# Small vectors loaded as rows, one product of eight on GpSimd, five inverses of eight on summed tiles, the MLP's flips in one PSUM tile, and a new order: a gated long convolution and a gMLP on one core

## The chip, the cores and the metric

The kernel runs on one core of one Trainium2 chip. The metric is the device time of one execution in microseconds (us); times of before are the median of three runs. Names in the profile: PE is TensorE (matmuls), PEld its weight loads, DVE VectorE, ACT ScalarE, POOL GpSimd, SP the engine that only issues DMAs; SPq and ACTq are their DMA issues.

## The reference

A block of two parts with adaptive layer norm (six modulation vectors sa, ca, ga, sb, cb, gb from `silu(c) @ w_mod`); S = 2048 rows, D = 640 channels, Fh = 864. All inputs are bfloat16.

```python
h = layernorm(x) * (1 + ca) + sa
k_shift = sum over t of k shifted by t rows * shift_k[:, t]      # four taps
kv = k_shift * v
y  = causal convolution of kv with ssm_k along S (by FFT)  +  kv * ssm_D
x  = x + ga * (h * y)
h  = layernorm(x) * (1 + cb) + sb
z  = gelu(h @ w_in);  z1, z2 = halves of z;  z2 = layernorm(z2)
g  = w_sp @ z2 + b_sp                                            # mixes the rows
x  = x + gb * ((z1 * g) @ w_out)
```

## The kernel before

**Stages.** The channels are cut into NU = 5 units u of 128. For each unit the filter (K side) and kv (U side) are transformed on TensorE: `stage1` (line 401 on) multiplies 16-row blocks with the small table F1 into a tile X1, `forward` (fwdK, fwdU) multiplies X1 with the tables M2, eight steps st per unit, each with six matmuls. A K step is copied to SBUF by ACT (khc, tile KH). A U step stays in PSUM (pu) and DVE multiplies it with KH into four partial products of 128x1024 elements (`prod`, line 457). The inverse (`inv`) multiplies with the tables G2 into pz, and a copy (zc) collects Z. For the steps in SUMS (1, 3, 5, 7) the partial products are written as float32 (tile Tf), two row sums (`csum`, line 466, POOL or DVE) reduce them to W, and the inverse takes six matmuls on W; for the other steps they are bfloat16 (tile T) and the inverse takes twelve on T.

Z of units 0 to 3 is transposed by one DMA (`zt`, line 673) into ZT, of which there is one buffer; four y steps (`y`, eight matmuls each, and `ym` on DVE) end it and multiply it into gh, the modulated layer norm of x (`ghm`, two operations for each unit and group of four row tiles, on POOL or DVE). `res` adds gh to x, `ln2` takes statistics for the second norm. Unit 4 is turned by PE instead (`zfl`, copies `zk`, then `yl`, `yml`).

**Inputs.** kv is made channel-wise: `ldk` loads k and v by DMA transpose (line 511), `diag` (line 528) makes four diagonal matrices from the four taps of a channel tile dt, `taps` multiplies with them, `tv` multiplies with v, `kvw` writes kv to DRAM, and `ldX` (line 386) reads filters (XK) and kv (XU) back in the layout of stage 1. Unit 0's XU needs both halves of dt0's write. ssm_D is added to XK (`addD`, line 396) from the tile D_col. D, the taps and c are loaded straight into partition layout, one element or four to a descriptor (lines 733, 736, 737).

**MLP.** Groups g of four row tiles. `zx` normalises, then group 0 (in two pieces p of two row tiles) is turned by PE (`hfl`) and modulated out of PSUM (`hmod`); groups 1 to 3 are turned by DMA (`turn`) and modulated in SBUF (`hmod2`). `zz` multiplies with w_in, `gelu` follows on ACT, `stz`, `agz`, `rstdz`, `zn` normalise z2. The mixing with w_sp (line 944) and the projection (line 965) come after, outside the list.

**The order.** Every operation is registered with `op(engines, kind, function, reads, writes)` and gets a number. The list ORDER names, in one line of text, which engine issues which number; an engine issues its own entries in the order of the list, and semaphores hold an instruction until its inputs and its buffer are there. SP's entries too run in their own order: a DMA whose input is late holds back those behind it. PSUM tags with their buffers: s1 (1), sm, pu, pz (2 each). FILLS are matmuls on the identity whose results nobody reads (`fill`, tag s1). `silut` and `gelut` are one-element activations that load ACT's tables for Silu (also used for the sines) and Gelu.

## Time and profile before

| | us |
|---|---|
| three runs | 325.06, 324.6, 325.04; median 325.04 |
| profiled execution, its time / its span | 324.96 / 323.0 |
| PE / DVE / ACT / POOL busy | 308.3 / 209.8 / 148.3 / 93.4 |
| first stage-1 block of U0 | starts at 26.03 |
| ZT transposes issued at | 60.07, 84.26, 99.69, 114.29 |
| first MLP matmul (zz) | starts at 136.16 |
| mixing with w_sp begins | 195.4 |

A span runs from the first to the last instruction; the execution's time is 2 us longer. A group line of the profile reads: line, engine, operation, tiles written <- read, shapes, count | busy us, mean ns of one | idle time of the engine before them and what ended it. In windows and in the list of instructions the first two numbers are start and length in us. Line 240 is the helper `mm`, line 243 the helper `copy`: their groups are told apart by the tiles.

### The profile page before, as it was taken

The numbers are of one execution on the slowest core, as the hardware profiler recorded it, in microseconds if no ns is written. First come the engines' busy times: TensorE is split into PE (matmuls) and PEld (weight loads), VectorE is DVE, ScalarE is ACT, GpSimd is POOL, SyncE is SP. The second block draws the span as 40 slices with busy tenths as digits, with TensorE's granted clock in tenths as the row PEclk, the third lists the DMA queues.
The fourth block names the chain that finished last, engine by engine and source line by source line (L and its number), as shares of the span: only waits on it lengthen the run. The fifth ranks groups of instructions, "written<-read, shape, count | busy, mean of one in ns | idle before, by whom it ended". The sixth has DMA issues, their size and how long they took to land.

```text
span 323.0 us, 6384 instructions
## 1 busy us (share of the span) xinstructions
PE 308.3 (95%) x2581; PEld 205.8 (64%) x2589; DVE 209.8 (65%) x464; ACT 148.3 (46%) x255; POOL 93.4 (29%) x121
## 2 busy tenths in 40 slices
PE   5969999899999998899999999999999999999996
PEld 2556879778889896655555555555555555555554
DVE  8967999999999998899676773433322222233333
ACT  4757999897779755397577683000000000000001
POOL 2440725559799898310111120000000000000000
PEclk9989999999999999999999999999999999999999
DMA  6999997996687876004308980567655555522231
GB/s 114 224 255 275 244 282 187 245 244 170 118 230 152 264 140 231 4 1 81 74 9 141 193 214 2 118 136 110 141 130 124 114 114 115 114 51 49 49 51 61
DMA packets 128868, 44.99 MB, mean 139 GB/s; under 512 B 117992, under 2 KB 128072, under 8 KB 128840
## 3 DMA queue, kind: packets, MB, share of 16 engines
q1 hardware_dynamic: 125672, 41.74, 59.0%
q10 hardware_dynamic: 3168, 2.86, 2.7%
q8 instruction: 20, 0.33, 0.4%
q14 instruction: 8, 0.07, 0.1%
HBM read 16.11 MB, written 5.24 MB: 66 GB/s over the span
## 4 chain that ended last, share of the span: by engine, by line
PE 76%; DMA 10%; DVE 7%; SPq 4%; issue 1%; ACT 1%; POOL 0%; POOLq 0%; DVEq 0%
PE ps L944 29%; PE pu L240 16%; PE pz L240 13%; PE po L965 9%; PE sm L240 5%; DMA ZT<-Z 5%; DMA X<-in_A_ssm_k_dram 5%; SPq L511 3%; PE s L240 3%; DVE Tf L457 1%; DVE X L243 1%; DVE st L570 1%; DVE T L457 1%; PE sm L823 0%; DVE big L543 0%
## 5 line engine op out<-in xcount | busy, mean ns | idle before, releaser
L944 PE MATMUL ps<-X,wT 128*128 128x432 bf16 x512 | 95.7, 346 | 0.0
L944 PEld LDWEIGHTS <-wT 128*128 128x128 bf16 x512 | 50.0, 98 | 42.2
L957 ACT COPY uT<-pt 128x896 bf16<-128x896 bf16 x1 | 0.9, 905 | 119.1 <-PE pt L956 119.1
L240 PE MATMUL pu<-X,M 128*128 128x128 bf16 (+1 forms) x480 | 47.1, 240 | 1.5 <-DVE T L457 0.9
L240 PEld LDWEIGHTS <-Z 128*128 128x128 bf16 x320 | 31.1, 98 | 26.6 <-DVE Z L832 0.4
L240 PEld LDWEIGHTS <-M 128*128 128x128 bf16 x480 | 37.8, 99 | 7.2 <-issue 1.8
L947 DVE SCALAR_TENSOR_TENSOR u<-ps,bcol,G 128x432 bf16<-128x432 f32 x18 | 12.0, 668 | 42.2 <-PE ps L944 42.2
L243 ACT CAST X<-s 128x1024 bf16<-128x1024 f32 x32 | 32.7, 1021 | 4.4 <-PE s L240 4.3
L965 PE MATMUL po<-w_o,uT 128*128 128x320 bf16 (+2 forms) x231 | 33.2, 295 | 0.1
L240 PE MATMUL pu<-big,Z 128*128 128x432 bf16 x160 | 32.8, 346 | 0.0
L466 POOL TENSOR_TENSOR W<-Tf 128x256 bf16<-128x256 f32 x38 | 28.0, 756 | 16.4 <-DVE Tf L457 15.6
L240 PE MATMUL pz<-big,Z 128*128 128x432 bf16 x160 | 32.6, 346 | 0.0
L947 DVE SCALAR_TENSOR_TENSOR u<-ps,bcol,M 128x432 bf16<-128x432 f32 x14 | 9.3, 667 | 30.2 <-PE ps L944 30.2
L965 PEld LDWEIGHTS <-uT 128*128 128x128 bf16 (+1 forms) x231 | 22.2, 98 | 9.9 <-issue 0.2
L240 PEld LDWEIGHTS <-G 128*128 128x128 bf16 x360 | 26.9, 98 | 1.9
L243 ACT CAST KH<-pu 128x512 bf16<-128x512 f32 x40 | 23.0, 595 | 6.7 <-PE pu L240 6.5
L457 DVE TENSOR_TENSOR Tf<-pu,KH 128x1024 f32<-128x1024 f32 x20 | 24.2, 1219 | 1.6 <-PE pu L240 1.1
L457 DVE TENSOR_TENSOR T<-pu,KH 128x1024 bf16<-128x1024 f32 x20 | 24.3, 1217 | 0.6 <-PE pu L240 0.5
L967 DVE TENSOR_TENSOR ot<-po,xt 128x320 bf16<-128x320 f32 (+1 forms) x33 | 15.9, 482 | 12.6 <-PE po L965 12.6
L243 ACT CAST Z<-pz 128x512 bf16<-128x512 f32 x35 | 20.3, 589 | 6.7 <-PE pz L240 6.4
L240 PEld LDWEIGHTS <-X 128*128 128x128 bf16 x288 | 18.1, 98 | 8.0 <-DVE X L396 4.5
L888 DVE BATCH_NORM_STATS2 stz<-X 128x6 f32<-128x432 bf16 x32 | 18.2, 594 | 7.1 <-ACT X L882 7.1
(143 smaller groups left out, 411.5 us busy)
## 6 DMA issues: line engine op xcount, KB each, us to landing
wm<-in_w_mod_dram SPq DMA_DIRECT2D x4, 800.0 KB, 5.6
out_dram<-ot SPq DMA_DIRECT2D x15, 160.0 KB, 2.3
big<-in_B_w_in_dram SPq DMA_DIRECT2D x2, 1080.0 KB, 8.3
X<-in_A_ssm_k_dram SPq DMA_DIRECT2D x4, 512.0 KB, 6.2
kv_scr<-big SPq DMA_DIRECT2D x4, 512.0 KB, 3.6
X<-kv_scr SPq DMA_DIRECT2D x4, 512.0 KB, 5.4
xt<-in_A_q_dram SPq DMA_DIRECT2D x3, 640.0 KB, 6.6
wm<-in_w_mod_dram ACTq DMA_DIRECT2D x2, 800.0 KB, 7.3
```

The costliest lines, as they stand in the source:

```text
L240: nc.tensor.matmul(o, lhsT=w, rhs=x, start=start, stop=stop)
L243: (e.copy if e is nc.scalar else e.tensor_copy)(dst, src)
L457: e.tensor_tensor(T_[:], tl[pu][:, :, :, None, :].to_broadcast([P, KP, 2, 2, DU]), tl[KH][:, :, None, :, :].to_broadcast([P, KP, 2, 2, DU] ...
L466: e.tensor_tensor(tl[W][:, :, o, :], T_[:, :, 0, o, :], T_[:, :, 1, 1 - o, :], op=ALU.add if o else ALU.subtract)
L511: e.dma_start_transpose(tl[name][:, o + h * m:o + (h + 1) * m], src[0, h * m:(h + 1) * m, dt * P:(dt + 1) * P])
L570: e.bn_stats(out=st[:, a, :], in_=xt[:, n, a * HS:(a + 1) * HS])
L888: op("D", "stz", lambda e, i=i, n=n, fc=fc: e.bn_stats(out=stz[:, n, fc, :], in_=tl[z2][:, i, fc * FC:(fc + 1) * FC]), r=[(z2, (i, fc))], ...
L944: nc.tensor.matmul(ps[:, :FC], lhsT=wTs[t][:, s_, :], rhs=tl["z2_%d" % (s_ // TB)][:, s_ % TB, fc * FC:(fc + 1) * FC], start=(s_ == 0), st ...
L947: nc.vector.scalar_tensor_tensor(u[:, sl], ps[:, :FC], bcol[:, t:t + 1], z1[t][:, sl], op0=ALU.add, op1=ALU.mult)
L957: nc.scalar.copy(uTs[t][:], pt[:])
L965: nc.tensor.matmul(ps[:, :hi - lo], lhsT=uTs[t][:fsz[ft], ft, :], rhs=w_o[:fsz[ft], ft, lo:hi], start=(ft == 0), stop=(ft == NFT - 1))
L967: nc.vector.tensor_tensor(ot[:, lo:hi], ps[:, :hi - lo], xt[:, t, lo:hi], op=ALU.add)
```

## The change

**Small vectors.** c, the taps and D are loaded as rows (5 x 128, 5 x 128 x 4, 80 x 8 elements, tag KH), turned by TensorE against the identity into PSUM (tag sm), and copied out; D is first widened on DVE or POOL into a zeroed tile of 80 x 128, so that its turned form has zeros where D_col had them. Silu reads c from PSUM. The memset of D_col goes.

**Steps.** MODE replaces SUMS: steps 0, 1, 3, 5, 7 of each unit are summed ("s"), 4 and 6 are not ("u"), and for step 2 ("p") ACT copies the forward tile pu to SBUF as float32 (`puc`) and POOL makes the product in bfloat16 (`prg`); its inverse takes twelve matmuls.

**Flips.** The five channel tiles of a piece of group 0 are turned into one PSUM tile (tag s1, one buffer) instead of five tiles of tag sm.

**Fills.** Seven (4, 2, 1, 1, 4, 1, 4 matmuls) instead of three (4, 1, 4).

**The list** is new. Entries by engine, before to after, where the numbers differ (the larger kinds):

| kind | before | after |
|---|---|---|
| prod | DVE 40 | DVE 35; puc ACT 5, prg POOL 5 |
| csum | POOL 38, DVE 2 | POOL 44, DVE 6 |
| ghm | POOL 27, DVE 13 | POOL 20, DVE 20 |
| res (units 0 to 3 and 4) | POOL 7, DVE 14 | POOL 3, DVE 18 |
| s1c | ACT 44, DVE 4 | ACT 41, DVE 7 |
| zc | ACT 35, DVE 5 | ACT 37, DVE 3 |
| zn | ACT 5, DVE 11 | ACT 7, DVE 9 |
| ln1 / xn | ACT 5, DVE 11 / ACT 4, DVE 12 | ACT 6, DVE 10 / ACT 3, DVE 13 |
| mneg, msgn, gneg, diag | POOL 2, 3, 3, 4; DVE 2, 1, 1, 1 | POOL 2, 4, 4, 3; ACT 2, 0, 0, 1; DVE 0, 0, 0, 1 |

Its start, decoded: SP before: D, taps, k and v of dt0 in halves (with XK0's second half between), x rows 0, k of dt1, XK1, kv write of dt0's second half, v of dt1, XU0, k of dt2. SP after: XK0's second half, D as rows, k and v of dt0 (first halves), XK1, k and v of dt0 (second halves), x rows 0, k of dt1, the kv write, v of dt1, XU0, k of dt2. ACT before: XK0's first half, silut, cosines, sines and copies, kv write of dt0's first half. ACT after: taps as rows, silut, XK0's first half, copy of the taps, dt0's diag (four multiplications), cosines, sines and copies, the same kv write. PE after: fill x4, turn of the taps, fill x2, turn of D, fill, taps dt0, fill, stage 1 of K0, of K1 (one block), taps dt0, the forwards of K0 with the other three blocks of K1 among them, taps dt1, stage 1 of U0. PE before had one block of K1 ahead of U0.

Its PE entries between the last y of a unit and the first y of the next:

| between | before | after |
|---|---|---|
| units 0 and 1 | 9 forwards, 4 stage-1, 2 u, 1 s, 3 taps | 7 forwards, 3 stage-1, 1 u, 1 p, 2 s, 1 taps |
| units 1 and 2 | 6 forwards, 4 stage-1, 3 u, 1 s, modulation columns | 7 forwards, 4 stage-1, 2 u, 3 s |
| units 2 and 3 | 7 forwards, 3 u, 3 s, modulation columns | 7 forwards, 2 u, 4 s, modulation columns |

(u, p, s: inverses of that kind.) In unit 4, after: inverse 4.0, inverse 4.3, forward 4.2, two more forwards, inverses 4.4, 4.5, 4.7, 4.6 with two forwards among them, y of unit 3, inverse 4.2, inverse 4.1; POOL meanwhile: a residual, row sums of 4.7 and 4.5, a gate operation, a row sum of 4.5, the product 4.2, a row sum of 4.1. Behind the last y of unit 3 come fill x4, fill x1 and the first yl; then, before the first hfl, fill x4. The first Gelu is behind two zx on ACT; `gelut`, which stood in unit 3, comes after 19 Gelus.

```diff
@@ -31,57 +31,58 @@
-FILLS = (4, 1, 4, )
-SUMS = (1, 3, 5, 7)
+FILLS = (4, 2, 1, 1, 4, 1, 4, )
+MODE = ('sspsusus', 'sspsusus', 'sspsusus', 'sspsusus', 'sspsusus')
 SLOTS = dict(Tf=2, W=2, X=3, X1=4, KH=9, T=3, Z=3, ZT=1, wm=1, big=2, dg=2, st1=2, s1=1, sm=2, pu=2, pz=2)
 PSUM_TAGS = ("s1", "sm", "pu", "pz")
 
 
 ORDER = """
...
 """
 
 
@@ -159,7 +160,6 @@
     x_nat = A_q[0].rearrange("(n p) d -> p n d", p=P)
     out_nat = out[0].rearrange("(n p) d -> p n d", p=P)
     ssm_fft = A_ssm_k.rearrange("(c g) (n f) -> (g n) c f", g=8, f=P)
-    d_fft = A_ssm_D.rearrange("(c g) -> g c", g=8)
     wmv = w_mod.rearrange("(t p) (j d) -> p t j d", p=P, j=6)
 
 
@@ -212,8 +212,6 @@
         gsa_bf = consta.tile([P, D], BF16)
         D_col = consta.tile([P, D // 8], BF16)
         sk = consta.tile([P, ND, 4], F32)
-        sk_bf = consta.tile([P, ND, 4], BF16)
-        c_bf = consta.tile([P, ND], BF16)
         sc = consta.tile([P, ND], F32)
         sc_rep = consta.tile([P, ND, P], BF16)
         sc_bf = consta.tile([P, ND], BF16)
@@ -266,7 +264,6 @@
         nc.gpsimd.iota(pint[:], [[0, 1]], base=0, channel_multiplier=1)
         nc.gpsimd.iota(pidx[:], [[0, 1]], base=0, channel_multiplier=1, allow_small_or_imprecise_dtypes=True)
         nc.gpsimd.iota(fidx[:], [[1, P]], base=0, channel_multiplier=0, allow_small_or_imprecise_dtypes=True)
-        nc.gpsimd.memset(D_col[:], 0.0)
         nc.gpsimd.iota(f1k[:], [[4, NKC], [0, 2]], base=1, channel_multiplier=0, allow_small_or_imprecise_dtypes=True)
         nc.gpsimd.iota(f1r[:], [[0, NKC], [16, 2]], base=48, channel_multiplier=0, allow_small_or_imprecise_dtypes=True)
         nc.gpsimd.memset(mpi[:], -2.0 * HALF_PI)
@@ -449,14 +446,20 @@
             pu, KH, T, pz, Z = "pu" + s, "KH" + s, "T" + s, "pz" + s, "Z%d" % u
             forward(pu, "X1U%d" % u, st)
 
-            summed = st in SUMS
-            ttag = "Tf" if summed else "T"
-
-            def product(e):
-                T_ = new(T, ttag, [P, KP, 2, 2, DU], F32 if summed else BF16)
-                e.tensor_tensor(T_[:], tl[pu][:, :, :, None, :].to_broadcast([P, KP, 2, 2, DU]),
-                                tl[KH][:, :, None, :, :].to_broadcast([P, KP, 2, 2, DU]), op=ALU.mult)
-            op("D", "prod", product, r=[pu, KH], w=[T], new=[(T, ttag)])
+            mode = MODE[u][st]
+            summed = mode == "s"
+            shape = [P, KP, 2, 2, DU]
+
+            def product(e, src=None):
+                T_ = new(T, "Tf" if summed else "T", shape, F32 if summed else BF16)
+                e.tensor_tensor(T_[:], (tl[pu] if src is None else tl[src])[:, :, :, None, :].to_broadcast(shape),
+                                tl[KH][:, :, None, :, :].to_broadcast(shape), op=ALU.mult)
+            if mode == "p":
+                uf = "uf" + s
+                op("A", "puc", lambda e: e.copy(new(uf, "T", [P, KP, 2, DU], F32)[:], tl[pu][:]), r=[pu], w=[uf], new=[(uf, "T")])
+                op("G", "prg", lambda e: product(e, uf), r=[uf, KH], w=[T], new=[(T, "T")])
+            else:
+                op("D", "prod", product, r=[pu, KH], w=[T], new=[(T, "Tf" if summed else "T")])
             W = "W" + s
             if summed:
                 def total(e, o):
@@ -730,16 +733,32 @@
                     resid(u, g, ns)
 
 
-        op("SA", "ldc", lambda e: e.dma_start(c_bf[:], c[0].rearrange("(t p) -> p t", p=P)), w=["c"])
+        identity()
+
+        def small_load(name, shape, src):
+            op("SA", "ld1", lambda e: e.dma_start(new(name, "KH", shape)[:], src), w=[name], new=[(name, "KH")])
+
+        def small_turn(name, r, fn):
+            def turn(e):
+                fn(new(name, "sm", [P, 512], F32))
+            op("P", "turn1", turn, r=r + ["ident"], w=[name], new=[(name, "sm")])
+        small_load("skr", [ND, P, 4], A_shift_k.rearrange("(t p) j -> t p j", p=P))
+        small_load("Dr", [D // 8, 8], A_ssm_D.rearrange("(c g) -> c g", g=8))
+        small_load("cr", [ND, P], c[0].rearrange("(t p) -> t p", p=P))
         op("A", "silut", lambda e: e.activation(warm[:], warm[:], ACT.Silu), w=["silut"])
-        op("A", "silu", lambda e: e.activation(sc[:], c_bf[:], ACT.Silu), r=["c", "silut"], w=["silu"])
-        op("S", "ldD", lambda e: e.dma_start(D_col[0:P:16, :], d_fft), w=["D"])
-        op("SA", "ldsk", lambda e: e.dma_start(sk_bf[:], A_shift_k.rearrange("(t p) j -> p t j", p=P)), w=["skb"])
-        op("D", "skc", lambda e: e.tensor_copy(sk[:], sk_bf[:]), r=["skb"], w=["sk"])
+        op("G", "dzero", lambda e: e.memset(new("Dw", "KH", [D // 8, P])[:], 0.0), w=["Dw"], new=[("Dw", "KH")])
+        op("DG", "dwide", lambda e: e.tensor_copy(tl["Dw"][:, 0:P:16], tl["Dr"][:]), r=["Dr"], w=["Dw"])
+        small_turn("tsk", ["skr"], lambda p_: [mm(p_[:, j * ND:(j + 1) * ND], tl["skr"][:, :, j], ident[0:ND, 0:ND], True, True)
+                                               for j in range(4)])
+        small_turn("tD", ["Dw"], lambda p_: mm(p_[:, 0:D // 8], tl["Dw"][:], ident[0:D // 8, 0:D // 8], True, True))
+        small_turn("tc", ["cr"], lambda p_: mm(p_[:, 0:ND], tl["cr"][:], ident[0:ND, 0:ND], True, True))
+        op("DA", "skc", lambda e: copy(e, sk[:].rearrange("p t j -> p j t"), tl["tsk"][:, 0:4 * ND].rearrange("p (j t) -> p j t", t=ND)),
+           r=["tsk"], w=["sk"])
+        op("DA", "dcol", lambda e: copy(e, D_col[:], tl["tD"][:, 0:D // 8]), r=["tD"], w=["D"])
+        op("A", "silu", lambda e: e.activation(sc[:], tl["tc"][:, 0:ND], ACT.Silu), r=["tc", "silut"], w=["silu"])
         index_bits(0, 2)
         f1_table()
         index_bits(2, 6)
-        identity()
         for dt in range(ND):
             load_kv(dt)
             short_conv(dt)
@@ -815,23 +834,25 @@
         def flip_piece(g, p, ns, xn2, hT):
             k, i0 = len(ns), ns[0] % TB
             for dt in range(ND):
-                pt, first = "ft%d_%d_%d" % (g, p, dt), dt == 0 and p == 0
+                pt, first = "ft%d_%d" % (g, p), dt == 0 and p == 0
 
                 def flips(e, dt=dt, pt=pt):
-                    p_ = new(pt, "sm", [P, k, P])
+                    if dt == 0:
+                        new(pt, "s1", [P, ND, k, P])
                     for i in range(k):
-                        e.transpose(p_[:, i, :], tl[xn2][:, i0 + i, dt * P:(dt + 1) * P], ident[:])
+                        e.transpose(tl[pt][:, dt, i, :], tl[xn2][:, i0 + i, dt * P:(dt + 1) * P], ident[:])
 
                 def modulate(e, dt=dt, pt=pt, first=first):
                     if first:
                         new(hT, "Z", [P, ND, TC])
-                    dst, src = tl[hT][:, dt, i0 * P:(i0 + k) * P], tl[pt][:].rearrange("p a b -> p (a b)")
+                    dst, src = tl[hT][:, dt, i0 * P:(i0 + k) * P], tl[pt][:, dt].rearrange("p a b -> p (a b)")
                     if e is nc.scalar:
                         e.activation(dst, src, ACT.Identity, bias=sb_col[:, dt:dt + 1], scale=cb1_col[:, dt:dt + 1])
                     else:
                         e.tensor_scalar(dst, src, cb1_col[:, dt:dt + 1], sb_col[:, dt:dt + 1], op0=ALU.mult, op1=ALU.add)
-                op("P", "hfl", flips, r=["ident"] + [(xn2, i0 + i) for i in range(k)], w=[pt], new=[(pt, "sm")], n=k)
-                op("AD", "hmod", modulate, r=[pt, "sb", "cb"] + ([] if first else [(hT, "new")]),
+                op("P", "hfl", flips, r=["ident"] + [(xn2, i0 + i) for i in range(k)] + ([(pt, "new")] if dt else []),
+                   w=[(pt, dt)] + ([] if dt else [(pt, "new")]), new=[] if dt else [(pt, "s1")], n=k)
+                op("AD", "hmod", modulate, r=[(pt, dt), "sb", "cb"] + ([] if first else [(hT, "new")]),
                    w=[(hT, (dt, p))] + ([(hT, "new")] if first else []), new=[(hT, "Z")] if first else [], n=k)
 
 

```

## The prediction

> **What bounds the kernel now.** I read the slices of the page first, then the windows of 10 us, the chain of waits, and last the timeline where PE stands still.
>
> ```profile
> PE   5969999899999998899999999999999999999996
> DVE  8967999999999998899676773433322222233333
> POOL 2440725559799898310111120000000000000000
> ...
> PE 76%; DMA 10%; DVE 7%; SPq 4%; issue 1%; ACT 1%; POOL 0%; POOLq 0%; DVEq 0%
> ```
>
> The slices are 8.1 us each. From slice 17 (137 us) to the end PE is full and no other engine is: the MLP, the token mixing and the projection are PE-bound, about 186 us, and nothing in the change touches their matmuls. What can move lies in the first 137 us, in three stretches: a start with holes in PE (slices 0 to 3), the five convolution units (4 to 15), and a hand-over to the MLP (16).
>
> ```profile
> 20.00:30.00 10.00, 8.78 (x58) 5.89 (x60) 7.13 (x17) 5.64 (x9) 1.36 (x2) 0.83 1.11 227
> 50.00:60.00 10.00, 10.00 (x122) 9.07 (x121) 9.86 (x17) 9.77 (x20) 5.43 (x9) 1.00 0.99 219
> 80.00:90.00 10.00, 9.89 (x125) 8.68 (x126) 10.00 (x18) 8.07 (x14) 7.62 (x9) 1.00 0.75 133
> ```
>
> Columns after the length: busy us of PE, weight loads, DVE, ACT, POOL, then the granted clock. In the units PE and DVE are both full at once, so taking work from one of them pays in part only. At 20 to 30 us neither is, and the clock is down at 0.83.
>
> ```profile
> 10.35 4.61 SPq L511 DMA_TRANSPOSE big<-in_A_k_dram  x1
> ...
> 14.99 0.58 SPq L386 DMA_DIRECT2D X<-in_A_ssm_k_dram  x1
> ...
> 20.86 0.61 PE L240 MATMUL s<-F1bd,X 128*128 128x256 bf16 x4 [2.32 <-DVE X L396]
> ```
>
> This is the hole: the second block of filters (XK1) is issued at 14.99, behind a transposing load that holds SP for 4.61 us. It lands at 20.55, and PE stands 2.3 us for it. After that twelve forward matmuls take 1.91 us where they take 0.88 later.
>
> **The change, part by part** (against the profiled execution: 324.96 us, span 323.0; the median 325.04 is 0.08 above it).
>
> *Start: -1.5.* SP sheds the loads of D (0.81) and the taps (0.77) and the 0.66 us by which its first issue (1.38) trails ACT's (0.72); it gains XK0's second half earlier (0.57) and one row load (nearest rows 0.35 to 0.44). So the first transposing load goes out near 0.72 + 0.57 + 0.4 = 1.7 instead of 3.07, 1.4 earlier. XK1 is listed ahead of the second half of k and v, thus near 5 us instead of 14.99, and three more stage-1 blocks of it (0.44 each) fill the wait before U0. Against this: ACT takes the tap copy and dt0's four diagonal products. ACT has no row for those; 4 x 0.19 (its 128x5 row) to 4 x 0.50 (its 128x256 sine) gives 0.8 to 2.0, I take 1.2, nearer the short end because 128 columns are half of 256. Behind them queue the table of cosines, eight sines, the stage-1 copies and ACT's issue of the first kv write. That write went out at 12.26; ACT's listed work before it now ends near 15. The other half's write went out at 15.71 and sat 2.07 in the queue, so the pair, which U0 needs whole, still comes slightly earlier. All in the first U block: bounds 0 (ACT eats it) and -3.8 (the hole, 2.5 with the idle after the last column, and 1.3 of slow clock behind it); I take what SP's head start shows, -1.5. The three extra early fills of 0.43 each at half clock lie before the first data.
>
> *Inverse with sums: -1.6.* Five items per unit are summed instead of four, and an unsummed inverse costs 12 matmuls against 6:
>
> ```profile
> 62.60 0.88 PE pz L240 x12
> ...
> 66.54 0.44 PE pz L240 x6
> ```
>
> 5 units x 0.44 = 2.2 us less PE. DVE loses five products (5 x 1.22 = 6.1) but takes over work from POOL: 4 row sums (0.42), 7 gate operations (0.43 to 0.53), 4 residuals (0.41), and 3 stage-1 copies from ACT (0.68); with the small moves its whole sum changes by -0.9 only. Bounds: 0 (DVE decides) and -2.2; I take -1.6, since the chain has PE at 76% and DVE at 7%.
>
> *One product on POOL: 0.* Rows that bound it:
>
> ```profile
> L457 DVE TENSOR_TENSOR T<-pu,KH 128x1024 bf16<-128x1024 f32 x20 | 24.3, 1217 | 0.6 <-PE pu L240 0.5
> ```
>
> POOL's row sums take 0.756 for 256 columns, its gate operations 1.16 to 1.19 for 512. For 1024: 2.0 if the straight line through both is drawn on, 3.0 at four row sums; I take 2 x 1.18 = 2.35, the nearer size. Five make 11.8; plus 6 row sums (4.5), minus 7 gate operations (8.3) and 4 residuals (4.8), and +0.5 of small moves: POOL +3.7 on 93.4. ACT's copy of the forward tile is 5 x 0.6 = 3.0. Cover: in units 1 to 3 the product is listed far ahead of its inverse. In unit 4 it is tight: between the start of inverse 4.0 and inverse 4.2, POOL has a residual, three row sums, a gate operation and the product, 1.19 + 3 x 0.76 + 1.18 + 2.35 = 7.0, and PE has five forward blocks, four summed inverses (0.44 each), two unsummed ones (0.88) and one y (0.2), 5.9. The missing 1.1 falls under PE's wait for the last transpose (below), so nothing is added; with 3.0 for the product and no such wait it is +1.8. Behind that inverse stand the last unit's Z and the whole hand-over.
>
> The Trainium skill speaks against this step: GPSIMD Engine Reference, section 4.1 (Engine selection), puts elementwise products on VectorE, GpSimd being about twice as slow for two inputs, and section 3.1 gives about 2.6 cycles an element. By that (an estimate, 1024 x 2.6 / 1.2 GHz) five would cost 11.1 instead of 11.8, and the forecast would not move. The trace agrees on the direction: 1.22 on DVE against 2.0 to 3.0.
>
> *The transposes of the units: +1.2.* Each unit's result goes through one DMA transpose into one buffer (ZT), so from the last y of a unit to the first y of the next PE has only what is listed between.
>
> ```profile
> 99.69 8.51 DMA ZT<-Z
> ...
> 114.29 8.47 DMA ZT<-Z
> ```
>
> From the end of one y to the start of the next these cost 8.63 and 8.60 us, the one of unit 1 10.36 (84.19 to 94.55). Listed PE work between, at 0.44 a block, 0.86 for taps, 0.77 for the modulation columns: before 10.5, 8.2, 7.8, and PE did wait 0.67 and 0.79. In the new list 7.9, 7.9 and 7.4. With 8.63, 8.63 and 8.60 the waits are 0.7 + 0.7 + 1.2 = 2.7 against 1.46: +1.2. Bounds: -1.5 (issued early enough to vanish) and +6.4 (10.36 each: 31.1 - 23.2 - 1.5). Behind the waiting y stand all of PE's forwards, and behind these DVE's products.
>
> *Flips in one PSUM tile: -0.3.* In the hand-over PE waited for a free buffer:
>
> ```profile
> 135.12 0.58 PE L823 MATMUL sm<-ident,Z 128*128 128x128 bf16 x4 [0.39 <-DVE Z L832]
> ...
> 136.04 0.27 PE L823 MATMUL sm<-ident,Z 128*128 128x128 bf16 x2 [0.34 <-ACT Z L830]
> ```
>
> Those waits go, but the first MLP matmul still needs the last of five modulations: a flip (0.28) and three in a row on DVE (0.41) make 1.5 against the 1.8 from 134.34 to 136.16. Bounds -1.3 (all gaps) and +0.5 (the second piece waits for the single buffer). Five more fills (5 x 0.21 = 1.1) are listed before the first yl, in place of a modulation product of 0.84 that moves behind it; if PE has no wait there they cost up to 1.1.
>
> *The Gelu table: +0.6.* The list puts the dummy Gelu that loads ACT's table behind some twenty real ones, where it stood in unit 3 before.
>
> ```profile
> L758 ACT ACT_TABLE_LOAD x1 | 1.3, 1283 | 0.0
> ```
>
> So the load falls to the first real Gelu, after two 0.92 us norms on ACT, with modulations of the second piece queued behind. Four PSUM buffers of 0.91 us each hold PE off; half of 1.28 is my price, bounds 0 and 1.3. The skill's page ScalarE: Activation LUTs (What ACT_TABLE_LOAD costs) adds a drain of 1.38 us to each switch; here the next ACT instruction began at 101.31, 1.30 after the load's start at 100.01, so this trace shows no drain. With it the term would be +1.3.
>
> Loads of c, the taps and D as rows turned by PE: three turns of a few columns and their copies, 1 us spread over PE, DVE and ACT in the start; they are in the start's bounds.
>
> Sum: -1.5 - 1.6 + 0 + 1.2 - 0.3 + 0.6 = **-1.6**, 323.4 on the profiled execution and, within its 0.08, on the median: **323.4**.
>
> **The rivals.**
> (a) *The transposes decide: slower.* Without their term the sum is -2.8. PE's covers are 23.2 us in all, so the gain is gone when the three average (23.2 + 1.46 + 2.8) / 3 = 9.1 us, between the 8.6 and 10.4 measured. At 9.8: 29.4 - 23.2 - 1.46 - 2.8 = +2.0, **327.0**. For it: the first of them did take 10.36, with other loads on the same queues. Against: two of three took 8.6 with two loads issued behind them.
> (b) *DVE is the bound and the change is hidden:* the list refills what DVE lost, DVE is at 9.9 to 10.0 in the windows; the gains of PE go into waits, **325.0**.
> (c) *The hole at 20 us closes whole:* -3.8 and -2.2 with ACT keeping up and the rest at 0: up to -6; I put the case at -5, **320.0**. Against: U0 hangs on the kv writes, one of which gets later.
>
> **How the numbers follow.** A run of this kernel tells from no change what is beyond 0.2%, 0.65 us. Forecast (a gain of 0.7 to 3.3) 0.45; (c) 0.13; (b) 0.14; (a), with the uncovered fills and the late ACT in it, 0.28. Faster 0.58, same 0.14, slower 0.28. The forecast's own range is 321.7 to 324.4. For eight in ten I go down to 319.6, just past (c), and up to 327.2, just past (a).
>
> **What would show it.** Start: XK1 issued before 7 us and the first U0 block before 25.5 (now 26.03). Inverses: 150 matmuls on summed tiles instead of 120 and 180 on unsummed ones instead of 240, blocks at 0.44 and 0.88 as before. Transposes: PE waits for ZT of 0.6 to 1.3 each. Flips: no wait of PE on modulations inside a piece. Table: one load next to the first Gelu. POOL: products of 2.0 to 3.0. The prediction is wrong if the first U0 block does not move, if a transpose takes 10 us three times, or if POOL's products are above 3 us, so that the inverses with them stop PE.

## The result and the profile after

The changed kernel takes 336.07 us (median of 337.72, 334.87, 337.27, 334.43) where the kernel before takes 324.93 beside it: a ratio of 1.0345, 95% interval 1.0281 to 1.0408. It is slower by 11 us; forecast were 323.4, with a range up to 327.2. The profiled execution is the one of 337.72 us (span 335.9), 12.8 above the 324.96 of the one shown before. Of the runs below, e7's median and ratio are of three executions: its fourth, of 343.37 us, fell into a slower state of the chip.

The slices of the changed kernel (8.4 us each), with the granted clock, and the first line of its chain of waits:

```profile
PE   6988889999997999679999999999999999999996
DVE  8999999999999999564874958253332223222333
POOL 3363846767695898210011113000000000000000
PEclk9999979999999999778999999999999999999999
...
PE 71%; DVE 16%; DMA 5%; ACT 3%; issue 2%; SPq 1%; POOL 0%; DVEq 0%; POOLq 0%; ACTq 0%
```

DVE's share of the chain has doubled from 7% to 16%. PE has new holes at slice 5 (42 us; slices count from 0), slice 12 (101 to 109 us) and slices 16 and 17 (134 to 151 us); the clock is down in slices 5 and 16 to 18. The windows of the same execution (start and length, then busy us of PE, weight loads, DVE, ACT, POOL, then the clock):

```profile
20.00:30.00 10.00, 8.51 (x68) 5.63 (x66) 9.34 (x19) 6.81 (x14) 2.85 (x3) 1.00 0.94 207
40.00:50.00 10.00, 7.51 (x66) 6.06 (x65) 9.46 (x19) 6.24 (x12) 5.16 (x7) 0.83 0.80 191
140.00:150.00 10.00, 5.82 (x35) 3.18 (x34) 6.48 (x22) 6.11 (x9) 1.30 (x2) 0.82 0.01 2
```

At 20 to 30 us the clock is now 1.00 (before: 0.83): the start did improve. At 140 to 150 PE is busy for 5.8 of 10 us, where the kernel before had all ten:

```profile
40.00:50.00 10.00, 9.95 (x99) 8.02 (x100) 9.52 (x27) 9.62 (x15) 3.52 (x5) 1.00 0.97 254
140.00:150.00 10.00, 10.00 (x64) 5.60 (x63) 9.79 (x35) 7.66 (x17) 1.25 (x2) 1.00 0.34 66
```

A ledger, by the start of the same work in both profiled executions: the first forward of unit 0 (step 3) 28.31 against 30.24, -1.9; the first stage-1 block of K2 51.30 against 48.35, so 4.9 lost in units 0 and 1; the first `yl` 132.95 against 129.12, another 0.9; the end of the MLP's first product 208.36 against 195.41, another 9.1. Everything behind it is the same. Three places are to be explained: 40 us, 99 us, and the hand-over at 135 to 154 us.

The hand-over in the list of instructions of the changed kernel (L843 flips, L850 and L852 modulations on ACT and DVE):

```profile
139.85 0.38 PE L843 MATMUL s<-ident,Z 128*128 128x128 bf16 x4
140.32 0.56 ACT L850 ACTIVATE Z<-s,sb_col,cb_col 128x256 bf16<-128x256 bf16 x1 [2.04 <-PE s L843]
140.92 0.41 DVE L852 TENSOR_SCALAR Z<-s,cb_col,sb_col 128x256 bf16<-128x256 bf16 x1 [2.24 <-ACT Z L850]
141.38 0.38 PE L843 MATMUL s<-ident,Z 128*128 128x128 bf16 x4 [1.15 <-DVE Z L852]
141.81 0.41 DVE L852 TENSOR_SCALAR Z<-s,cb_col,sb_col 128x256 bf16<-128x256 bf16 x1 [0.48 <-PE s L843]
142.25 0.56 ACT L850 ACTIVATE Z<-s,sb_col,cb_col 128x256 bf16<-128x256 bf16 x1 [1.37 <-DVE Z L852]
142.87 0.27 PE L843 MATMUL s<-ident,Z 128*128 128x128 bf16 x2 [1.10 <-ACT Z L850]
```

On this tile only one of the three engines is at work at any time. DVE's modulation at 140.92 reads what PE had finished at 140.2, and yet it was released by ACT's, which reads another block of the same PSUM tile; the next flips write blocks that nobody reads, and were released by DVE's. The releasers are read from semaphore events, so the rows show how the program was made to wait, although the list registers the blocks one by one (`(pt, dt)` in the diff); whether the chip would need it no run shows. From the first flip to the last modulation 3.8 us pass; before it was 2.4 (134.34 to 136.77), with ACT and DVE side by side:

```profile
134.34 0.39 PE L823 MATMUL sm<-ident,Z 128*128 128x128 bf16 x4
134.66 0.41 DVE L832 TENSOR_SCALAR Z<-sm,cb_col,sb_col 128x256 bf16<-128x256 bf16 x1 [0.46 <-PE sm L823]
134.82 1.63 ACT L830 ACTIVATE Z<-sm,sb_col,cb_col 128x256 bf16<-128x256 bf16 x3 [0.57 <-PE sm L823]
```

And the clock, in the MLP's product of the changed kernel, five matmuls of 432 columns at 144 and five at 153 us:

```profile
144.26 2.01 PE L238 MATMUL pz<-big,Z 128*128 128x432 bf16 x5
...
153.44 1.08 PE L238 MATMUL pu<-big,Z 128*128 128x432 bf16 x5
```

One after the other they come every 0.36 us at first and every 0.18 us later: half clock. The granted clock of the same execution, in windows of 0.1 us, is 0.5 in four stretches and 1.0 around them: 44.0 to 47.4 us, 136.1 to 139.6, 143.0 to 146.4 and 149.8 to 153.2, each 3.4 us long. In the 3.4 us ahead of each PE was busy for 0.9, 2.9, 1.1 and 1.5 us: three of the four follow a stretch in which PE mostly waited, and the one at 136 us follows matmuls of 16 columns. The kernel before has one such stretch ahead of the mixing with w_sp, at 21.6 to 25.0 us.

This divides the 9.1 us of the hand-over. From the first `yl` to the mixing PE idles 4.7 us where it was 1.1, 3.6 more; a modulation product of 0.7 us stands behind the first `yl` now; the rest, nearly 5 us, is what PE does not get done in the three stretches at half clock, at most 1.7 us each.

The place at 40 us, in the changed kernel (L583 to L585 finish the first LayerNorm statistics, one to six columns each; L531 builds the diagonals of the taps):

```profile
37.07 2.10 POOL L469 TENSOR_TENSOR W<-Tf 128x256 bf16<-128x256 f32 x3 [1.04 <-DVE Tf L455]
38.54 0.65 DVE L584 TENSOR_TENSOR sums<-mv 128x1 f32<-128x1 f32 x1
39.13 1.04 POOL L531 TENSOR_TENSOR dg<-ident,sk 128x512 bf16<-128x512 bf16 x1
39.22 0.96 DVE L585 TENSOR_TENSOR mv<-mv,sums 128x1 f32<-128x1 f32 x1
40.30 0.16 DVE L584 TENSOR_TENSOR sums<-mv 128x3 f32<-128x3 f32 x1
40.38 1.04 POOL L531 TENSOR_TENSOR dg<-ident,sk 128x512 bf16<-128x512 bf16 x1 [0.21 <-PE sm L238]
40.49 0.94 DVE L585 TENSOR_TENSOR mv<-mv,sums 128x3 f32<-128x3 f32 x1
41.96 1.21 DVE L455 TENSOR_TENSOR T<-pu,KH 128x1024 bf16<-128x1024 f32 x1
43.22 0.60 PE L238 MATMUL pu<-X,M 128*128 128x256 bf16 x6 [2.49 <-DVE T L455]
```

Such an operation takes 0.16 us when POOL is idle and 0.65 to 0.96 when POOL is at work, and then it ends within 0.02 us of POOL's instruction (38.54 + 0.65 = 39.19 and 37.07 + 2.10 = 39.17; 39.22 + 0.96 = 40.18 and 39.13 + 1.04 = 40.17). DVE is held until POOL is done, its product comes late, and PE stands 2.49 us. DVE's products themselves, which read one side from PSUM, are not held: 1.21 us beside POOL's product as elsewhere.

The same at 99 us, beside POOL's new product, which is 2.13 us long:

```profile
99.17 2.13 POOL L455 TENSOR_TENSOR T<-T,KH 128x1024 bf16<-128x1024 f32 x1
99.22 2.37 DVE L689 TENSOR_TENSOR xt<-xt,gh 128x512 bf16<-128x512 bf16 x1
...
102.24 0.76 PE L238 MATMUL sm<-sc_bf,wm 128*128 128x1 bf16 x25 [0.72 <-DVE gh L669]
103.97 0.39 PE L238 MATMUL sm<-Ebd,ZT 128*128 128x64 bf16 x8 [0.96 <-DVE gh L669]
```

The residual sum takes 0.41 elsewhere, 2.37 here, and ends 0.29 us behind POOL's product. Behind it on DVE queue the multiplications of the y blocks (L669), and PE waits for their PSUM tiles twice.

This is a rule of the Trainium skill that I had not weighed: SBUF — State Buffer, section "SBUF: two separate sides", says that VectorE and GpSimd share a pair of SBUF ports as "an exclusive lock, not a bandwidth split", taken by a VectorE instruction with two SBUF inputs against a GpSimd one that reads SBUF, and held for the whole instruction. The rows above agree, the products with one PSUM input included.

### The profile page after: what moved, and what is told of

Read it like the earlier page. It is cut to its first block, busy times and chain, and to the rows that moved or that the text cites. A ratio compares the mean times of both kernels' runs of the same rounds, so it can differ in the third digit from the quotient of the medians.

```text
span 335.9 us, 6411 instructions
## 1 busy us (share of the span) xinstructions
PE 315.7 (94%) x2573; PEld 207.2 (62%) x2573; DVE 217.0 (65%) x473; ACT 153.1 (46%) x269; POOL 98.7 (29%) x122
## 4 chain that ended last, share of the span: by engine, by line
PE 71%; DVE 16%; DMA 5%; ACT 3%; issue 2%; SPq 1%; POOL 0%; DVEq 0%; POOLq 0%; ACTq 0%
PE ps L965 28%; PE pu L238 14%; PE pz L238 12%; PE po L986 9%; PE sm L238 5%; DVE Tf L455 3%; PE s L238 3%; DMA ZT<-Z 2%; DMA big<-in_A_v_dram 2%; DVE big L546 1%; DVE T L455 1%; SPq L383 1%; DVE gh L669 1%; DVE X L241 1%; DVE gh L652 1%
## 5 line engine op out<-in xcount | busy, mean ns | idle before, releaser
L238 PE MATMUL pu<-X,M 128*128 128x128 bf16 (+1 forms) x480 | 46.1, 240 | 4.3 <-DVE T L455 2.8
L238 PEld LDWEIGHTS <-Z 128*128 128x128 bf16 x320 | 32.2, 101 | 28.8 <-issue 2.9
L469 POOL TENSOR_TENSOR W<-Tf 128x256 bf16<-128x256 f32 x44 | 33.0, 768 | 25.1 <-DVE Tf L455 14.4
L238 PE MATMUL pz<-big,Z 128*128 128x432 bf16 x160 | 33.8, 358 | 0.0
L241 ACT CAST X<-s 128x1024 bf16<-128x1024 f32 x30 | 30.8, 1027 | 4.0 <-PE s L238 3.8
L455 DVE TENSOR_TENSOR Tf<-pu,KH 128x1024 f32<-128x1024 f32 x25 | 30.1, 1214 | 1.7 <-PE pu L238 1.7
L238 PEld LDWEIGHTS <-G 128*128 128x128 bf16 x330 | 24.9, 98 | 2.4 <-issue 0.3
L241 ACT CAST Z<-pz 128x512 bf16<-128x512 f32 x37 | 21.5, 601 | 6.1 <-PE pz L238 6.0
L238 PEld LDWEIGHTS <-X 128*128 128x128 bf16 x288 | 18.8, 100 | 6.7 <-issue 1.1
L238 PE MATMUL sm<-big,dg 128*128 128x512 bf16 (+1 forms) x80 | 21.1, 392 | 0.9 <-DVE big L546 0.7
```

Source lines behind the costliest of these rows:

```text
L238: nc.tensor.matmul(o, lhsT=w, rhs=x, start=start, stop=stop)
L241: (e.copy if e is nc.scalar else e.tensor_copy)(dst, src)
L455: e.tensor_tensor(T_[:], (tl[pu] if src is None else tl[src])[:, :, :, None, :].to_broadcast(shape), tl[KH][:, :, None, :, :].to_broadcast ...
L469: e.tensor_tensor(tl[W][:, :, o, :], T_[:, :, 0, o, :], T_[:, :, 1, 1 - o, :], op=ALU.add if o else ALU.subtract)
```

## The experiments

Theories at the outset: A, instructions that touch one PSUM tile run in turn, and this starves PE at the hand-over; C, DVE held by POOL makes the holes in the units. Rivals: B, the hand-over is late because its inputs and the clock are; D, time won in the units is lost at the next wait. All medians stand beside the kernel before in the same runs.

| run | median us | before | difference | ratio, 95% |
|---|---|---|---|---|
| changed kernel | 336.07 | 324.93 | +11.1 | 1.0281 to 1.0408 |
| e1 flips apart | 334.92 | 325.32 | +9.6 | 1.0202 to 1.0342 |
| e1b flips first | 331.46 | 325.32 | +6.1 | 1.0096 to 1.0234 |
| e2 before, one tile | 330.39 | 325.32 | +5.1 | 1.0042 to 1.0242 |
| e5 diagonals later | 335.85 | 325.32 | +10.5 | 1.0197 to 1.0364 |
| e3 table early | 337.86 | 325.22 | +12.6 | 1.0326 to 1.0417 |
| e4 product on DVE | 338.40 | 325.22 | +13.2 | 1.0366 to 1.0482 |
| e6 three list moves | 328.85 | 325.22 | +3.6 | 1.0068 to 1.0129 |
| e7 step 0 unsummed | 336.38 | 325.22 | +11.2 | 1.0318 to 1.0425 |
| e8 residual later | 327.12 | 325.13 | +2.0 | 1.0037 to 1.0094 |
| e9 apart, in order | 328.62 | 325.13 | +3.5 | 1.0069 to 1.0115 |
| e10 one fill | 326.42 | 325.13 | +1.3 | 1.0015 to 1.0043 |
| e11 table late | 326.85 | 325.82 | +1.0 | 1.0007 to 1.0050 |
| e12 finish early | 326.81 | 325.82 | +1.0 | 1.0000 to 1.0038 |
| e13 all of these | 327.37 | 325.82 | +1.5 | 1.0018 to 1.0061 |
| e14 two tiles | 326.76 | 325.49 | +1.3 | 0.9997 to 1.0051 |

**e2, the one tile alone.** The kernel before, with the flips of the change.

```diff
-                pt, first = "ft%d_%d_%d" % (g, p, dt), dt == 0 and p == 0
+                pt, first = "ft%d_%d" % (g, p), dt == 0 and p == 0
...
-                    p_ = new(pt, "sm", [P, k, P])
+                    if dt == 0:
+                        new(pt, "s1", [P, ND, k, P])
```

> The kernel before with nothing but the one PSUM tile for a piece's flips; list and numbering unchanged. Theory A: 3 to 7 us slower, 328 to 332. Rival B, that the tile as such costs nothing: 324.5 to 325.5. My prediction's own term was -0.3 with bounds of -1.3 and +0.5.

Measured +5.1 (1.4 to 7.9 by the interval), within theory A; up to the hand-over the profiled execution is at most 0.6 us away from the kernel before's. Its flips, in the list of instructions:

```profile
135.92 0.27 PE L824 MATMUL s<-ident,Z 128*128 128x128 bf16 x2 [0.50 <-DVE Z L833]
136.28 0.56 ACT L831 ACTIVATE Z<-s,sb_col,cb_col 128x256 bf16<-128x256 bf16 x1 [1.45 <-PE s L824]
136.89 0.27 PE L824 MATMUL s<-ident,Z 128*128 128x128 bf16 x2 [0.70 <-ACT Z L831]
137.20 0.56 ACT L831 ACTIVATE Z<-s,sb_col,cb_col 128x256 bf16<-128x256 bf16 x1 [0.36 <-PE s L824]
137.82 0.27 PE L824 MATMUL s<-ident,Z 128*128 128x128 bf16 x2 [0.65 <-ACT Z L831]
```

PE flips, ACT modulates, PE flips: 0.92 us a block, where blocks in two tiles overlapped. The first MLP product starts at 138.91 (before: 136.16) and runs at half clock. The tile also went to tag s1, which has one buffer; that this is not the cause shows in e1b, which keeps it.

**e1 and e1b, in the changed kernel.** e1 puts the old flip block back, with its entries in the list moved where they must be (copies of the last modulation rows behind their products, two modulations of the second piece earlier). e1b keeps the one tile and lists the flips first:

```diff
-P766 D738 P772 A767 D773 P768 P774 D775 G778 A769 S759 P770 D771
+P766 P772 P768 P774 P770 D738 A767 D773 D775 G778 A769 S759 D771
...
-P782 P784 A823 A783 P786 D697 D701 D698 P788 A789 D700 P790
+P782 P784 P786 P788 P790 A823 A783 D697 D701 D698 A789 D700
```

> The changed kernel with each flip block back in a PSUM tile of its own (the two copies of the last modulation rows move up to free those tiles, and two modulations of the second piece move up). Theory A, that flips and modulations of one PSUM tile run strictly in turn and that this starves PE at the hand-over: the flips of the first piece take about 2 us in place of 5 and 326 to 331 us result, 5 to 10 under the changed kernel's 336.1. Rival B, that the hand-over is late because its inputs and the clock are: 335 to 337.

> The changed kernel with the one PSUM tile kept and the five flip blocks of a piece listed ahead of all its modulations. Theory A in the form 'any two instructions on the tile run in turn, whatever their order': the flips run back to back without waiting for a modulation, the five modulations are still in sequence, 331 to 335 us. If only the order of the list made the waits (modulations then overlap on ACT and DVE): 328 to 331. Rival B: 335 to 337.

e1 gained 1.5 beside the kernel before, less than A asked for (326 to 331): in this list five tiles in two buffers make PE wait too, 0.49 us for each pair, and its second piece stood 2.32 us behind ACT, which had the table load and two Gelus in front of the modulations. e1b gained 5.0 and is what A said in its weaker form:

```profile
138.68 1.23 PE L843 MATMUL s<-ident,Z 128*128 128x128 bf16 x10
139.99 0.56 ACT L850 ACTIVATE Z<-s,sb_col,cb_col 128x256 bf16<-128x256 bf16 x1 [2.42 <-PE s L843]
140.59 0.73 DVE L852 TENSOR_SCALAR Z<-s,cb_col,sb_col 128x256 bf16<-128x256 bf16 x2 [2.62 <-ACT Z L850]
...
141.35 0.56 ACT L850 ACTIVATE Z<-s,sb_col,cb_col 128x256 bf16<-128x256 bf16 x1 [0.80 <-DVE Z L852]
141.95 0.41 DVE L852 TENSOR_SCALAR Z<-s,cb_col,sb_col 128x256 bf16<-128x256 bf16 x1 [0.63 <-ACT Z L850]
```

The ten flips go through in one run; the five modulations are still in a row, ACT behind DVE behind ACT, 2.4 us in all. So it was less the tile than the tile together with a list that alternates on it. B falls as the whole story: nothing was done to inputs or clock, and 5 us came back.

PSUM — Partial Sum Buffer in the Trainium skill, section "PSUM bank collisions raise a hardware error", says that PSUM is to be guarded by bank and not by address, ScalarE against VectorE included; I had not weighed that either. The rows go one step further than a bank of its 2 KiB: the fifth block of a piece begins at byte 2048 of the tile, and its modulation keeps its turn with the others all the same (in the changed kernel it is the one at 141.81, and ACT's of the second block, at 142.25, waits for it).

**e5, the place at 40 us.** POOL's two diagonal builds go behind the reciprocal root that follows the finish.

```diff
-G225 G72 A547 D548 G60 P254 A255 ... G541
+G225 A547 D548 P254 A255 ... G541 G72 G60
```

> The changed kernel with POOL's two diagonal builds of the short convolution (taps 3 and 4) listed after the first rstd, so that they no longer run beside DVE's finish of the first LayerNorm statistics. Theory C, that a DVE instruction that overlaps a POOL instruction is held until that ends: the finish's small instructions fall from 0.4-0.96 us to about 0.2, the PE gap of 2.65 us at 40 us mostly closes, 333 to 334.5 us. Rival D, that the time gained there is lost again at the next wait in units 0 and 1: 335.5 to 336.5.

```profile
38.61 0.64 DVE L584 TENSOR_TENSOR sums<-mv 128x1 f32<-128x1 f32 x1
39.28 0.16 DVE L585 TENSOR_TENSOR mv<-mv,sums 128x1 f32<-128x1 f32 x1
...
41.70 0.60 PE L238 MATMUL pu<-X,M 128*128 128x256 bf16 x6 [0.91 <-DVE T L455]
```

The step at 39.2 takes 0.16 for 0.96, PE's wait falls from 2.49 to 0.91, and the first block of K2 starts at 48.44, 2.9 us earlier. That much of C is shown. The whole time does not follow: C had 333 to 334.5, and the median lies where rival D put it. The profiled execution took 332.74 at a mean clock of 0.989, the other three 335.5 to 336.4 at 0.973 to 0.980. At equal clock there is a gain (332.74 against the changed kernel's 334.43 at 0.989, 335.49 against 337.27 and 337.72 at 0.980), of 1.7 to 2.2 us, but these are single runs.

**e3, e4, e7, single parts.** e3 puts the entry of the Gelu table (A132) back into the middle of the units. e4 takes product 2 back to DVE, from PSUM, without ACT's copy, and its entries in the list go from POOL's to DVE's. e7 leaves step 0 unsummed, so that four steps are summed, as before the change.

```diff
-                op("A", "puc", lambda e: e.copy(new(uf, "T", [P, KP, 2, DU], F32)[:], tl[pu][:]), r=[pu], w=[uf], new=[(uf, "T")])
-                op("G", "prg", lambda e: product(e, uf), r=[uf, KH], w=[T], new=[(T, "T")])
+                op("A", "puc", lambda e: None)
+                op("D", "prg", product, r=[pu, KH], w=[T], new=[(T, "T")])
```

```diff
-MODE = ('sspsusus', 'sspsusus', 'sspsusus', 'sspsusus', 'sspsusus')
+MODE = ('uspsusus', 'uspsusus', 'uspsusus', 'uspsusus', 'uspsusus')
```

> The changed kernel with the instruction that loads the Gelu table moved up to where the kernel before has it, in the middle of the units. If the 1.28 us table load ahead of the first Gelu sat on the path of the hand-over: -0.6 to -1.3, so 334.8 to 335.5 us. If ACT has that time to spare there, or PE's wait is filled by something else: within 0.3 of the changed kernel.

> The changed kernel with product 2 of each unit back on DVE, read from PSUM, in the place where ACT made its float32 copy; no copy, nothing of it on POOL. My prediction put the product on POOL at 0 (+1.8 if uncovered). Theory C (DVE held by POOL, 2.13 us a product): DVE gets 5 products of 1.22 back and loses five stretches in which it is held, 1 to 3 us faster than the changed kernel, 333 to 335. Rival: DVE was the bound of the units and is now fuller by 6 us: 337 to 341.

> The changed kernel with step 0 of each unit unsummed again (four summed steps in place of... three summed and one on POOL of eight, as many sums as before less one): its ten sums on POOL and DVE go away, its product is written as bfloat16, and each unit's inverse takes 12 matmuls in place of 6 there. The prediction's term said that summing saves 0.44 us of PE a unit, so going back costs +2.2 on PE: 337 to 339. If instead the sums hold DVE and POOL up (DVE instructions waiting for POOL's), going back is free or gains: 333 to 336.

None of the three gains. e3 is 1.5 worse beside the kernel before, at clocks of 0.975 to 0.984; the load lay at 100.4 us as planned, so alone it is not the loss. e4 is 2.1 worse, where C had 333 to 335 and its rival 337 to 341: DVE, fuller by five products, costs more than POOL's product does, though the residual sum is back at 0.41. e7 (three runs) is level by its median and 0.8 worse by the middle of its ratio (1.0371 against 1.0345). The intervals of all three overlap the changed kernel's, so these are directions at most, not sizes.

**e6, e8, e10, the moves together.** e6 joins e1b, e3 and e5. e8 adds a move of the held residual sum (unit 0, group 2) behind the last y block of unit 1. e10 adds a cut of the fill before the flips.

```diff
-P444 A460 G413 D615 A393 P360 ... G418 D419 P632 D633 D634
+P444 A460 G413 A393 P360 ... G418 D419 P632 D633 D615 D634
...
-FILLS = (4, 2, 1, 1, 4, 1, 4, )
+FILLS = (4, 2, 1, 1, 4, 1, 1, )
```

> The changed kernel with three moves in the list alone: flips of a piece ahead of its modulations, the Gelu table load back in the middle of the units, the two diagonal builds after the first rstd. If the three losses are separate, 331.5 less 0.6 to 1.3 for the table less 1 to 3 for the hole at 40 us: 327 to 330. If time gained in the units is lost at the next wait, 330.5 to 331.5.

> The three list moves again, and a fourth: DVE's residual sum of unit 0, group 2 (xt<-xt,gh, 2.39 us there beside POOL's product of unit 3, 0.41 elsewhere) listed after the last y block of unit 1. Theory C, that POOL's product holds DVE there and so makes PE wait 0.90 and 1.13 us behind the y blocks: that sum takes 0.4 again, both waits go, 1.3 to 2.5 us under the three moves' 328.85: 326.3 to 327.5. Rival: the time is lost again at the next transpose of Z that PE waits for (1.23 us there): 328 to 329.

> The four list moves with one filling matmul in place of four ahead of the first flips. If the four, which ran at half clock (1.87 us), only delay the flips: 0.5 to 1.2 us faster than the four moves. If they keep up the clock of what follows: slower by 0.5 to 2.

+3.6, +2.0 and +1.3, each as its theory had it, though from e6 to e8 and from e8 to e10 the intervals overlap. In e8 DVE beside POOL's product, from its list of instructions:

```profile
98.20 2.13 POOL L455 TENSOR_TENSOR T<-T,KH 128x1024 bf16<-128x1024 f32 x1
98.23 0.68 DVE L669 TENSOR_TENSOR gh<-gh,sm 128x512 bf16<-128x512 bf16 x1
99.25 1.22 DVE L455 TENSOR_TENSOR Tf<-pu,KH 128x1024 f32<-128x1024 f32 x1 [0.34 <-ACT KH L241]
```

With work that reads PSUM in its place, nothing is held beside the product, and both waits of PE behind the y blocks are gone; 5.9 us pass from the first to the last y block of unit 1, 7.7 in the changed kernel. PE found a new wait at once, 1.07 us by its row for ACT's stage-1 copy (1.24 in the expectation of e11). In e10 one fill took 0.38 us where the four of e6 took 1.87, at half clock: it fits that they stood in the way of the flips more than they helped.

**e9, e11 to e14, what is left.** e9 is e8 with tiles apart, two alive at a time. e11 moves the table load to where ACT is idle ahead of the hand-over, e12 the finish of the statistics ahead of POOL's sums, e13 does both and cuts the fill before the first `yl`; all on e10. e14 is e11 with the first piece's flips in two tiles, one for ACT and one for DVE.

```diff
-                        new(pt, "s1", [P, ND, k, P])
+                        new(pt, "sm" if two else "s1", [P, ND - 3 * two, k, P])
```

> As the run before it (four list moves), but the flips of a piece in a PSUM tile of their own each, two alive at a time, listed flip, flip, modulation, flip, modulation and so on, and the copies of the last modulation rows moved up to free those tiles. Theory A in the form 'modulations of one PSUM tile run one after the other on ACT and DVE, those of two tiles side by side': the five modulations of the first piece take 1.6 to 2.0 us in place of 2.4, 0.5 to 1.5 us faster than the one tile with flips first. If the one tile costs nothing once the flips come first: equal within 0.5; if the two copies on ACT cost more than that: slower by 0.5 to 1.

> The four list moves with one fill, and the Gelu table load moved again: from 97.8 us, where ACT's next stage-1 copy is late and PE then waits 1.24 us for it, to just ahead of the hand-over, where ACT is idle for 4.3 us. If the load is what made that copy late: the wait of 1.24 goes and 0.4 to 1.2 us with it, 325.2 to 326.0. If DVE's late product makes PE wait there anyway: 326.2 to 326.6, no change.

> The four list moves with one fill, and DVE's finish of the first LayerNorm statistics listed ahead of the two sums of unit 0, step 5, on POOL that it still overlaps (0.40 and 0.64 us in place of 0.16 each). If DVE held by POOL is still what makes PE wait 1.08 us at 41.75: 0.5 to 1.0 us faster, 325.4 to 325.9. Rival: the finish then waits for ACT's statistics and holds DVE longer: 326.4 to 327.5.

> Both of the last two moves together, and one filling matmul in place of four ahead of the last unit's blocks too. If the three are separate: 324.0 to 325.2, level with the kernel before (325.1). If the fills there keep up the clock of the hand-over, 326 to 328.

> The kernel with the table load ahead of the hand-over, and the five flips of the first piece in two PSUM tiles: column blocks 0, 1, 2 in one, modulated by ACT, 3 and 4 in the other, modulated by DVE. Theory A (modulations of one tile in sequence): ACT's three run one after the other (about 1.8 us), DVE's two beside them; in place of 2.4 us for all five in one row, 0.4 to 0.8 us faster than 326.85 where the kernel before takes 325.82, so 0.2 to 0.7 above that kernel. If the tile no longer matters: 1.0 above it.

e9 missed: the modulations did overlap and the clock stayed at 1.00 from 130 to 150 us, but ACT had two more copies in the hand-over and the whole was 1.5 slower than e8. In the profile it is behind the first `yl`: 69.3 us from there to the mixing, 67.6 in e11, both at a clock of 1.00; which wait it is stays open. e11 closed the wait for ACT's stage-1 copy at 100 us, and one of 1.15 behind DVE's product opened at 107; e12 brought the finish forward into other sums of POOL's (0.65, 0.64, 0.31 us for its steps). Both +1.0, so neither is a cause by itself. e13 gained nothing more: +1.5, in the range that its expectation gives for fills that keep up the clock (326 to 328), and its runs have a median clock of 0.990 where e11's have 0.994 and e12's 0.995. e14 did what A says of two tiles:

```profile
135.82 0.73 DVE L854 TENSOR_SCALAR Z<-sm,cb_col,sb_col 128x256 bf16<-128x256 bf16 x2 [0.76 <-PE sm L845]
136.08 1.48 ACT L852 ACTIVATE Z<-s,sb_col,cb_col 128x256 bf16<-128x256 bf16 x3 [1.42 <-PE s L845]
```

ACT's three and DVE's two run side by side, 1.74 us in all for 2.4. The whole did not follow: +1.3, where A had 0.2 to 0.7. Four of its twelve runs took 325.1 to 325.7 at a clock of 0.994 to 1.0, level with the kernel before, and eight 326.5 to 327.4 at 0.988 to 0.993. No version beat the kernel before.

## Why the prediction was wrong

*Start, -1.5:* right in kind, a little small. XK1 is issued at 4.83 us (forecast: before 7, before the change 14.99), the first U0 block starts at 23.88 (forecast: before 25.5, before the change 26.03), 2.15 earlier. The hole did not close whole, so rival (c) falls.

*Inverse with sums, -1.6:* the counts are right, 150 and 180 matmuls, in blocks as long as before. What they are worth in time stays open: e7 gives 0 to 0.8 for going back, within scatter, and 1.9 at equal clock (336.36 and 336.38 against 334.43 at 0.989, few runs), so the 1.6 is neither confirmed nor refuted. DVE's sum was booked at -0.9 there, but the items named come to +2.3 to +3.0 ahead of the small moves, which are not listed; DVE's busy time rose by 7.2 us (209.8 to 217.0), of which 4.3 is the holding of the next paragraph.

*One product on POOL, 0:* POOL's product takes 2.13 us, in the bounds of 2.0 to 3.0. The step failed elsewhere: its cover was sought for the inverse that waits for the product, and each engine's duration was taken as its own. What POOL does lengthens what DVE does meanwhile. Beside POOL a residual sum cost 2.37 for 0.41, and the finish of the statistics 2.3 more in all (0.40, 0.65, 0.96 and 0.94 for 0.16 each). The same holding was in the profile of before, a step of the finish at 0.94 us, and was not looked for. That DVE took residual sums and gates over from POOL, booked at 0.41 to 0.53 each, put more such instructions beside it. As a place for product 2 POOL was still the better one: taken back to DVE it cost more (e4).

*Transposes, +1.2:* wrong in sign. PE idles 0.43 us for ZT in the whole execution, at the first y of unit 2 (before: 0.67 and 0.79). From the end of the last y to the start of the first y 7.8, 8.4 and 8.2 us pass, where 8.6 was forecast for each, and PE works in 7.75, 8.01 and 7.65 of them, about what was listed (7.9, 7.9 and 7.4). The transposes were shorter, 6.7 to 8.3 us from issue to landing against 8.5 to 9.7 before, so the work covers them; why they were shorter stays open. Rival (a) had the sign of the result and not its cause.

*Flips in one PSUM tile, -0.3 (bounds -1.3 and +0.5):* the step that failed most. It counted the waits for a free buffer as gone and took flips and modulations of different blocks of one tile as free of each other, and it said that PE would not wait inside a piece. They run in turn: PE waits 1.15 and 1.10 us in the first piece and again in the second. Alone, in the old list, this cost 5.1 us (e2; 1.4 to 7.9 by the interval), ten times its upper bound; in the new list undoing the alternation brought 5.0 back (e1b).

*Fills, up to 1.1:* that was for those ahead of `yl`, and cutting them did not pay (e13). The four ahead of the flips, which the kernel before has too, were not priced; at half clock they lasted 1.80 us, and cutting three gave 0.7 (e10), within the intervals.

*Gelu table, +0.6:* the load does stand at the first real Gelu, at 145.65 us. Alone it was not worth anything measurable (e3); in e1 it lay in front of the second piece.

*No term at all for the clock.* The new holes were followed by PE at half clock. Runs of one kernel (e8) go from 326.06 at a mean clock of 1.000 to 329.79 at 0.990, those of e14 from 325.09 at 1.000 to 327.35 at 0.988, those of e12 from 326.26 at 1.000 to 327.00 at 0.990, so a hundredth of clock goes with 0.7 to 3.7 us. I added and subtracted waits one by one, and what the clock does behind them was in none of the terms. What lowers it at 136 us stays open: the waits just there are under 0.6 us, the matmuls ahead of it are of 16 columns in the kernel before too, and with nearly the same list it was 0.83 in that window in e10 and 1.00 in e9 and e11.

Of the 11.1 us then, each step beside the kernel before: 5.0 by the alternation on the tile (e1b), 2.5 by DVE held at 40 us with the table (e6), 1.6 by the one residual sum (e8), 0.7 by the fills (e10), all with the slow clock behind them. That is 9.8. Only the first of these steps, and the way from +11.1 to +1.3 as a whole, are clear of the intervals; how the rest divides is a direction. The last 1.3 has no single cause that these runs show, since a wait that was closed came up elsewhere (e11), but it has a place: in e11's profiled execution, at a clock of 1.00 there, 67.6 us pass from the first `yl` to the mixing, 66.1 before, with a wait of 1.01 for modulations that still run in a row and the 0.7 us of the moved product. With these faults mended (e10) the new list is 1.8 us ahead at the first forward of unit 0, 0.2 at the first `yl`, and behind at the end: the start's gain is used up in the units, where PE and DVE are both near full; which waits use it up was not tested.

## What to carry to other kernels

In this kernel a PSUM tile is the unit of waiting: work that should overlap on ACT, DVE and PE belongs in tiles of its own, and where it must share one, all writes are listed ahead of all reads. Work given to POOL isn't free to DVE: look for DVE instructions that end when a POOL instruction ends or just behind it, and put those with an input in PSUM beside POOL's long ones. A tuned order depends on every duration in it, so a change to one tile must be priced with the order around it, and a new wait of PE with the slow clock that follows.

## What was not expected of the hardware

DVE is held to the end of a POOL instruction, even for one column: 0.96 us for 0.16. PE ran at exactly half clock (0.36 us for 0.18 a matmul of 432 columns) for stretches of 3.4 us, in e13 for 6.8 (130.3 to 137.1), though no single wait of PE ahead of them was longer than 2.5 us. In the changed kernel the four filling matmuls at 138 us ran at half clock themselves; behind them, at 139.6, the clock was back, and the waits of the flips lost it again at 143.0. The table load delayed ACT by its 1.28 us and by nothing more (before: load at 100.01, next instruction at 101.31).
